# Query loads for two groups at once, with the output store ahead of them and the key loads behind them, all in SyncE's queue

## The chip, the cores and the metric

The kernel runs on one core of one Trainium2 chip. The metric is the device time of one execution in microseconds (us); the program is launched once, and there is no arithmetic on the host. A core has five engines that matter here: PE (TensorE, matrix products; its weight loads are shown as PEld), DVE (VectorE), ACT (ScalarE), POOL (GpSimd) and SP (SyncE, which only issues transfers). Transfers between HBM and SBUF, and the transposes of 16-bit tiles from SBUF to SBUF, are run by 16 DMA engines. SP issues them through one hardware queue (q1 in the profile), ACT through another (q10).

## What is computed

```python
# q: 4 x 12288 x 128, kv: 4 x 384 x 32 x 128, all float32
kv_pool = kv.reshape(B, H // 4, 4, W // 4, 4, C).mean(axis=(2, 4))
k = v = kv_pool.reshape(B, -1, C) @ w_sr            # 4 x 768 x 128
s = (q @ k.transpose(0, 2, 1)) / np.sqrt(C)
a = np.exp(s - s.max(-1, keepdims=True))
a /= a.sum(-1, keepdims=True) + 1e-09
x = (a @ v).reshape(4 * 12288, 128)
h = x @ w_in                                        # 1024 wide
e = np.exp(h - h.max(-1, keepdims=True))
solu = h * e / (e.sum(-1, keepdims=True) + 1e-09)
mu, var = solu.mean(-1, keepdims=True), solu.var(-1, keepdims=True)
out = ((solu - mu) / np.sqrt(var + 1e-06) * g_ln) @ w_out
```

An attention over 768 pooled keys, and behind it a feed-forward layer with a SoLU and a layer norm, for each of 49,152 tokens.

## The kernel before

The tokens are cut into 384 tiles of 128. Four tiles make a group (96 groups), 96 tiles make one image of the batch (4 images). One Python loop over 384 slots writes the whole program out; each engine runs its instructions in the order in which this loop emits them, so that order is set by hand. In slot t the loop emits different stages of several tiles at once:

- tile t: the scores `s` on PE (`scores_pe`, L587), their maximum on DVE, the exponential on ACT (`scores_exp`), and the split of the result into two 16-bit halves `phl` (`scores_split`), the last step of which is a DMA transpose of `phl` into `pT` (L622) that SP issues;
- the group whose last tile was two slots earlier starts its weighted sum of the values, `xa` (`values`, L647). Its products read all four `pT` of the group, so the fourth transpose of a group is the one that is needed soonest;
- tile t-10: the hidden layer `h` (L700), its maximum (`junkd`, L708), its exponential `e` (L724), the product `u` (L738), the square sum (`junk`, L803);
- tile t-11: `u` in two 16-bit halves on POOL (`uhl`, L755 and L762) and their transpose into `uT` (L777, SP);
- tile t-14: the last product `o` (L828), which reads `uT`; for every fourth tile the output `ob` (L851, DVE) and its store (L860, SP).

The queries of a group are one load of 128 x 512 floats (256 KB) into `qf` (`q_load`, L528, SP; three buffers). It is issued at the end of the last slot of each group, three groups ahead.

The keys of image b+1 are summed up while image b is worked on: 16 positions `pos`, each one load `kv_load` (L227) of 128 x 768 floats (384 KB) into `kv`, and for `pos` above 0 two additions on POOL into `ka` (`kv_add`, L238), one for each half. `kv_plan` gives the slot of each step. Of the image that follows the first, six loads are issued by SP at the start (`SOON`); the other 42 loads of the kernel are issued by ACT, in a slot that is a multiple of four. Of these the two of table `LATE` have slots of their own. From slot 70 of an image on, the steps of `key_steps` make the keys and values of the next image out of `ka`.

The order in which all this reaches SP is shown with the change. SP works through its queue strictly in order: a transfer whose input is not ready holds all that stand behind it. At most eight transfers of both queues are under way, since each waits for the one that used its semaphore eight transfers earlier.

The functions that the diff touches, and those that call them:

Of the kernel before, what the change touches and what calls it, by code (L numbers as in the profile page):

```python
# [11 lines left out]
F32 = mybir.dt.float32  # L12
# [9 lines left out]
P = 128  # L22
# [9 lines left out]
GT = 4  # L32
# [11 lines left out]
LO = 14  # L44
# [17 lines left out]
FIT_AT = 302  # L62

SOON = {0: (), 1: (8, 8), 2: (8, 8), 3: (27, 33), 4: (39, 45), 5: (51, 54)}
LATE = {6: (12, 16, 18), 7: (16, 20, 22)}


@with_exitstack
def kernel(
# [15 lines left out]
    nc = tc.nc  # L85

    dmt = ctx.enter_context(tc.tile_pool(name="dmt", bufs=2))
# [59 lines left out]
    state = {}  # L147
# [351 lines left out]
    def kv_plan(b):  # L499


        for pos in range(RR):


            if b == 1 and pos in SOON:
                for half, slot in enumerate(SOON[pos]):
                    yield slot, [partial(kv_add, b, half, pos)]
                continue
            slot = 6 * pos - (28 if b == 1 else 30)
            load, *adds = (slot // GT * GT, slot + 3, slot + 5)  # L510
            if b == 1 and pos in LATE:
                load, *adds = LATE[pos]
            yield load, [partial(kv_load, b, pos)]
            if pos:
                for half, add in enumerate(adds):
                    yield add, [partial(kv_add, b, half, pos)]
        for slot, half, *fs in key_steps(b):
            yield slot, [partial(f, b, half) for f in fs]


    QL = 1

    def q_load(g):
        if g >= NG or g % QL:
            return
        b, gb = divmod(g, GPB)
        t = dmt.tile([P, QL * 512], F32, tag="qf", name=f"qf_{g}", bufs=3)
        nc.sync.dma_start(t, qT[b, :, gb * 512 : (gb + QL) * 512])  # L528
        state["qf", g // QL] = t

    def by_tile(a):
        return a.rearrange("p (t j) -> p j t", j=GT)
# [4 lines left out]
    def wide(g):  # L537
        return g < GPB or g >= NG

    def q_scale(g):  # L540
        if wide(g) or NG <= g:
            return
        qf = state["qf", g // QL][:, (g % QL) * 512 : (g % QL + 1) * 512]
        nc.gpsimd.tensor_scalar(
# [3 lines left out]
    def q_split(g):  # L548
        if NG <= g < NG + GPB:
            return  # L550
        qf = state["qf", g // QL][:, (g % QL) * 512 : (g % QL + 1) * 512]
        if wide(g):
# [292 lines left out]
        nc.gpsimd.tensor_tensor(f, f2, state.pop(("v3", g)), op=ALU.add)  # L845
        nc.gpsimd.tensor_tensor(f2, f, mhalf[:, :GT], op=ALU.pow)

    def final_out(g, to=None):
        _, f = state["f", g]
        ob = dmt.tile([P, GT, P], F32, tag="ob", name=f"ob_{g}")  # L850
        nc.vector.scalar_tensor_tensor(  # L851
            ob,
            state["po", g].rearrange("p (j c) -> p j c", j=GT),
            swi,
            f.unsqueeze(2).to_broadcast([P, GT, P]),
            op0=ALU.mult,
            op1=ALU.mult,
        )
        rows = out[g * GT * P : (g + 1) * GT * P, :] if to is None else to
        nc.sync.dma_start(rows.rearrange("(p j) c -> p (j c)", j=GT), ob.rearrange("p j c -> p (j c)"))  # L860

# [32 lines left out]
    for n in range(16):  # L894
        if n == OUT_AT:
            nc.sync.dma_start(raw_out, w_out.bitcast(I32))
        if n == Q_AT:
            q_load(0)
        kv_first_load(*divmod(n, 8))
    q_load(1)  # L900
    for pos in SOON:
        kv_load(1, pos, nc.sync)
    nc.scalar.mul(w_sr16, wsr, 1.0 / RR)
# [157 lines left out]
    def at_last(t, fn, *args):  # L1061

        if 0 <= t < NT and t % GT == GT - 1:
            fn(t // GT, *args)
# [13 lines left out]
    for slot in range(NT):  # L1078
        i = slot - LH
# [50 lines left out]
        if slot < NT - 1:  # L1130
            at(slot - LO, final_pe)
        at(i - 1, hidden_turn)
        if slot % GT == GT - 1:
            q_load(slot // GT + 3)
        at_last(slot - LO - 1, final_out)
        at_last(slot - XSP, values_out)
        for st in todo:
            if st[0].func is kv_add:
# [96 lines left out]
    def general():  # L1235

        for b in range(B):
# [4 lines left out]
            for n in range(16):  # L1242
# [4 lines left out]
                t = dmt.tile([P, NK], F32, tag="kvc", name=f"kvg_{kb}_{n}", bufs=9)  # L1247
# [9 lines left out]
            kv_now(kb, kv_v_pe, kv_v_out, kv_v_high, kv_v_low)  # L1257
            g = kb * GPB
            with tc.For_i(0, GPB, 1) as i:
                qf = dmt.tile([P, 512], F32, tag="qf", name=f"qf_{g}", bufs=3)  # L1260
                nc.sync.dma_start(qf, qT[b, :, bass.ds(i * 512, 512)])
                state["qf", g] = qf
                q_split(g)
                q_low(g)
                for t in range(g * GT, g * GT + GT):
                    scores_pe(t)
                    scores_exp(t)
                    scores_split(t)
                for n in range(8):
                    values(g, n // 2, n % 2)  # L1270
                values_out(g)
                values_split(g)
                values_norm(g)
                values_recip(g)
                values_recip_u(g)
                for t in range(g * GT, g * GT + GT):
                    hidden_pe(t)
                    hidden_max(t)
                    hidden_exp(t)
                    hidden_u(t)  # L1280
                    hidden_high(t)
                    hidden_low(t)
                    hidden_turn(t)
                    hidden_var(t)
                    final_pe(t)
                final_scale(g)
                final_root(g)
                final_out(g, to=out[bass.ds(b * NTOK + i * 512, 512), :])
# [39 lines left out]
```

## Time and profile before

| what | us |
|---|---|
| median of 3 runs | 1852.11 |
| lowest and highest of them | 1843.84, 1857.69 |
| the profiled execution, its own time | 1843.65 |
| its span (first to last instruction) | 1841.9 |
| PE busy in it | 1818.3 |
| DVE, ACT, POOL busy | 1761.9, 1742.6, 1667.2 |

The profiled execution took 1.75 us more than its span, and it is 8.5 us under the median of the unprofiled runs, at their lower end. Busy times overlap, since the engines work beside each other. An engine's busy share is an average; which engine holds a stretch up is read from the chain of waits, and from how far apart the same step of two groups that follow each other stands.

### The profile page before, as it was taken

Reading aid. Unit: us, or ns where it says so; the run is one execution under the profiler, and the core shown is the slowest. Engines: PE = TensorE matmul, PEld = TensorE weight load, DVE = VectorE, ACT = ScalarE, POOL = GpSimd, SP = SyncE. Lnnn points to the kernel's source line nnn. Section 1 sums busy time; section 2 is a strip of 40 time slices with the busy share of each in tenths; the row PEclk is TensorE's granted clock in tenths of the full one; section 3 lists DMA queues with packets and bytes.
Section 4 is the critical chain, followed back from the end, with each engine's and each line's share of the span. In section 5 each row is a group of like instructions: output and inputs, shape, how many; then the busy total and the mean of one; then the engine's idle time right before and its main releaser. Section 6 shows DMA issues by size and latency. Waiting matters only on the chain.

```text
span 1841.9 us, 42770 instructions
## 1 busy us (share of the span) xinstructions
PE 1818.3 (99%) x15747; PEld 1218.5 (66%) x15747; DVE 1761.9 (96%) x2635; ACT 1742.6 (95%) x3129; POOL 1667.2 (91%) x1466
## 2 busy tenths in 40 slices
PE   8999999999999999999999999999999999999998
PEld 5577777777666666666666666666666666666666
DVE  6999999999999999999999998999999999999997
ACT  5999999999999999999999998999999999999997
POOL 5899999899999999989999998998988988888887
PEclk9999999999999999999999999999999999999999
DMA  9999999999999999999999999999999999999997
GB/s 301 203 249 230 230 253 232 247 230 237 242 241 241 246 245 242 246 235 235 247 239 241 242 222 230 247 239 224 222 233 230 232 235 231 220 235 224 230 223 168
DMA packets 1440027, 432.80 MB, mean 235 GB/s; under 512 B 1404608, under 2 KB 1408832, under 8 KB 1439552
## 3 DMA queue, kind: packets, MB, share of 16 engines
q1 hardware_dynamic: 1433616, 413.45, 112.6%
q10 hardware_dynamic: 6192, 16.52, 3.2%
q8 instruction: 126, 2.06, 0.5%
q14 instruction: 93, 0.76, 0.1%
HBM read 52.50 MB, written 25.17 MB: 42 GB/s over the span
## 4 chain that ended last, share of the span: by engine, by line
PE 46%; DVE 26%; ACT 15%; issue 9%; DMA 2%; POOL 1%; SPq 0%; DVEq 0%; ACTq 0%; POOLq 0%
PE o L828 13%; PE h L700 13%; PE s L587 10%; PE xa L647 10%; DVE junkd L708 8%; DVE phl L619 6%; DVE nm L608 5%; ACT e L724 4%; ACT junk L803 4%; DVE u L738 3%; ACT phl L611 3%; ACT s L609 2%; DVE ob L851 2%; DVE xl L659 2%; DMA kv<-in_kv_dram 1%
## 5 line engine op out<-in xcount | busy, mean ns | idle before, releaser
L762 POOL TENSOR_TENSOR uhl<-u,uhl 128x1024 f16<-128x1024 f32 x382 | 815.0, 2134 | 32.3 <-ACT uhl L753 0.6
L828 PEld LDWEIGHTS <-uT 128*128 128x128 f16 x9072 | 537.9, 98 | 89.1 <-issue 0.9
L828 PE MATMUL o<-wch,uT 128*128 128x128 f16 x6048 | 568.1, 219 | 0.1
L828 PE MATMUL o<-wcl,uT 128*128 128x128 f16 x3024 | 526.1, 219 | 0.0
L738 DVE SCALAR_TENSOR_TENSOR u<-h,rz,e 128x1024 f32<-128x1024 f32 x384 | 490.4, 1277 | 33.3 <-ACT e L724 32.7
L708 DVE TENSOR_SCALAR_CACHE_REDUCE junkd<-h,rz 128x1024 bf16<-128x1024 f32 x384 | 490.7, 1278 | 7.6 <-PE h L700 7.2
L647 PE MATMUL xa<-pT,vhl 128*128 128x512 f16 x1728 | 470.4, 380 | 5.4 <-DMA pT<-phl 5.4
L755 POOL TENSOR_SCALAR uhl<-u 128x1024 f16<-128x1024 f32 x379 | 395.8, 1044 | 83.9 <-DVE u L738 72.7
L724 ACT ACTIVATE e<-h,nm,rz 128x1024 f32<-128x1024 f32 x384 | 458.5, 1194 | 8.2 <-DVE junkd L708 8.2
L803 ACT ACTIVATE junk<-u,su 128x1024 bf16<-128x1024 f32 x384 | 438.0, 1141 | 0.1
L609 ACT ACTIVATE s<-s,nm 128x768 f32<-128x768 f32 x384 | 334.7, 872 | 47.6 <-DVE nm L608 47.1
L619 DVE SCALAR_TENSOR_TENSOR phl<-s,phl 128x768 f16<-128x768 f32 x384 | 365.8, 953 | 6.5 <-ACT phl L611 4.1
L608 DVE TENSOR_REDUCE nm<-s 128x1 f32<-128x768 f32 x384 | 360.1, 938 | 9.1 <-PE s L587 4.6
L611 ACT ACTIVATE phl<-s 128x768 f16<-128x768 f32 x384 | 311.1, 810 | 12.1
L700 PEld LDWEIGHTS <-xh 128*128 128x128 f16 x1536 | 144.0, 97 | 195.4 <-issue 27.1
L647 PEld LDWEIGHTS <-vhl 128*128 128x128 f16 x1728 | 162.4, 98 | 141.3 <-issue 16.0
L700 PE MATMUL h<-w_in_h,xh 128*128 128x512 f16 x768 | 228.9, 380 | 3.6 <-DVE rz L682 3.2
L700 PE MATMUL h<-w_in_l,xh 128*128 128x512 f16 x768 | 229.0, 380 | 0.0
L700 PE MATMUL h<-w_in_h,xl 128*128 128x512 f16 x768 | 228.8, 380 | 0.0
L587 PEld LDWEIGHTS <-qh 128*128 128x128 f16 x1152 | 122.6, 114 | 42.9
L587 PE MATMUL s<-kh,ql 128*128 128x384 f16 x576 | 140.8, 326 | 0.1
L587 PE MATMUL s<-kl,qh 128*128 128x384 f16 x576 | 140.8, 326 | 0.0
(153 smaller groups left out, 1820.4 us busy)
## 6 DMA issues: line engine op xcount, KB each, us to landing
qf<-in_q_dram SPq DMA_DIRECT2D x96, 256.0 KB, 3.8
out_dram<-ob SPq DMA_DIRECT2D x96, 256.0 KB, 2.9
kv<-in_kv_dram ACTq DMA_DIRECT2D x42, 384.0 KB, 4.3
kv<-in_kv_dram SPq DMA_DIRECT2D x22, 384.0 KB, 7.5
pT<-phl SPq DMA_TRANSPOSE x384, 4.0
uT<-uhl SPq DMA_TRANSPOSE x378, 4.6
raw_in<-in_moe_w_in_dram SPq DMA_DIRECT2D x1, 1024.0 KB, 5.1
raw_out<-in_moe_w_out_dram SPq DMA_DIRECT2D x1, 1024.0 KB, 9.6
```

Source lines behind the costliest of these rows:

```text
L587: nc.tensor.matmul(s[:, half, :384], tokens(lh)[:, j, :], rh[:, half * 384 : (half + 1) * 384], start=n == 0, stop=n == 2,)
L608: nc.vector.tensor_reduce(nm, s, axis=AX.XY, op=ALU.max, negate=True)
L619: nc.vector.scalar_tensor_tensor(phl[:, 1], state.pop(("s", t)), SC, phl[:, 0], op0=ALU.mult, op1=ALU.subtract)
L647: nc.tensor.matmul(xa, v[:, c, :], pT[:, :, a * NKC + c, :], start=n == 0, stop=n == len(seq) - 1)
L700: nc.tensor.matmul(h[:, hs], lh[:, ts], rh[:, hs], start=n == 0, stop=n == 2)
L708: nc.vector.tensor_scalar(junk, state["h", t], state["rz", g][1][:, j : j + 1], None, op0=ALU.mult, op1=ALU.min, accum_out=nm,)
L724: nc.scalar.activation(e, state["h", t], AF.Exp, bias=nm, scale=state["rz", g][0][:, js], accum_out=state["z2", g][:, js],)
L738: nc.vector.scalar_tensor_tensor(u, state.pop(("h", t)), state["rz", g][2][:, j : j + 1], state.pop(("e", t)), op0=ALU.mult, op1=ALU.mult, ...
L755: nc.gpsimd.tensor_scalar(uhl[:, 0, :], u, 1.0, 1.0, op0=ALU.mult, op1=ALU.mult)
L762: low.tensor_tensor(uhl[:, 1, :], u, uhl[:, 0, :], op=ALU.subtract)
L803: nc.scalar.activation(junk, u, AF.Square, scale=-float(DFF), bias=su, accum_out=state["v3", g][:, j : j + 1],)
L828: nc.tensor.matmul(po[:, ts], uT[:, a * NFC + c, :], w[:, c, :], start=start, stop=stop)
```

## The change

Queries are loaded for two groups at once (`QL = 2`; 512 KB, 128 x 1024 floats, two buffers in the place of three), every eight slots, at slot 8n+3. The store of a group's output is taken out of `final_out` and emitted one slot later, so that it stands directly ahead of the query load (and in the other half of the groups at the same place, with no load behind it). The loads of the keys are all issued by SP, in the same slots, one or two of them directly behind the query load; `kv_plan` moves some of the additions of `ka` two slots later, so that they stay at least four slots behind their load, and the two rows of `LATE` get other slots. The first two groups' queries are still loaded separately, into two halves of one tile.

```diff
-LATE = {6: (12, 16, 18), 7: (16, 20, 22)}
+LATE = {6: (11, 16, 18), 7: (19, 22, 24)}
...
             slot = 6 * pos - (28 if b == 1 else 30)
-            load, *adds = (slot // GT * GT, slot + 3, slot + 5)
+            load = (slot - 2) // (2 * GT) * 2 * GT + GT - 1
+            first = max(slot + 3, load + GT)
+            adds = first, first + 2
             if b == 1 and pos in LATE:
                 load, *adds = LATE[pos]
-            yield load, [partial(kv_load, b, pos)]
+            yield load, [partial(kv_load, b, pos, nc.sync)]
...
-    QL = 1
+    QL = 2
...
-        t = dmt.tile([P, QL * 512], F32, tag="qf", name=f"qf_{g}", bufs=3)
+        t = dmt.tile([P, QL * 512], F32, tag="qf", name=f"qf_{g}", bufs=2)
...
+    def q_first_load(g):
+        if g == 0:
+            state["qf", 0] = dmt.tile([P, QL * 512], F32, tag="qf", name="qf_0", bufs=2)
+        nc.sync.dma_start(
+            state["qf", 0][:, g * 512 : (g + 1) * 512], qT[0, :, g * 512 : (g + 1) * 512]
+        )
...
-    def final_out(g, to=None):
+    def final_out(g, to=None, later=False):
...
+        state["ob", g] = ob
+        if not later:
+            final_store(g, to)
+
+    def final_store(g, to=None):
+        ob = state.pop(("ob", g))
         rows = out[g * GT * P : (g + 1) * GT * P, :] if to is None else to
         nc.sync.dma_start(rows.rearrange("(p j) c -> p (j c)", j=GT), ob.rearrange("p j c -> p (j c)"))
...
-            q_load(0)
+            q_first_load(0)
...
-    q_load(1)
+    q_first_load(1)
...
-        if slot % GT == GT - 1:
-            q_load(slot // GT + 3)
-        at_last(slot - LO - 1, final_out)
+        at_last(slot - LO - 2, final_store)
+        if slot % (2 * GT) == GT - 1:
+            q_load(slot // GT + 4)
+        at_last(slot - LO - 1, partial(final_out, later=True))
```

In SyncE's queue, in the second image before the change, a row `pT_8210` is one of the four transposes of one group's `phl` (the number is that of the buffer's tile), and `uT`, `out_dram`, `qf` are the transfers named above:

```order
L860 DMA out_dram<-ob_8106 128x512
L622 DMA_TRANSPOSE pT_7919<-phl_8112 128x12x128
L777 DMA_TRANSPOSE uT_8176<-uhl_8128 128x16x128
L528 DMA qf_8178<-in_q_dram 128x512
L622 DMA_TRANSPOSE pT_8210<-phl_8183 128x12x128
L777 DMA_TRANSPOSE uT_8244<-uhl_8196 128x16x128
L622 DMA_TRANSPOSE pT_8210<-phl_8252 128x12x128
L777 DMA_TRANSPOSE uT_8322<-uhl_8269 128x16x128
L622 DMA_TRANSPOSE pT_8210<-phl_8331 128x12x128
L777 DMA_TRANSPOSE uT_8393<-uhl_8343 128x16x128
L860 DMA out_dram<-ob_8395 128x512
L622 DMA_TRANSPOSE pT_8210<-phl_8401 128x12x128
```

The store stands directly ahead of the fourth `pT` of each group, and the query load directly ahead of the first; the same place in the queue after the change:

```order
L875 DMA out_dram<-ob_7787 128x512
L631 DMA_TRANSPOSE pT_7890<-phl_7863 128x12x128
L786 DMA_TRANSPOSE uT_7924<-uhl_7876 128x16x128
L631 DMA_TRANSPOSE pT_7890<-phl_7932 128x12x128
L786 DMA_TRANSPOSE uT_8002<-uhl_7949 128x16x128
L631 DMA_TRANSPOSE pT_7890<-phl_8011 128x12x128
L786 DMA_TRANSPOSE uT_8073<-uhl_8023 128x16x128
L631 DMA_TRANSPOSE pT_7890<-phl_8080 128x12x128
L786 DMA_TRANSPOSE uT_8144<-uhl_8096 128x16x128
L875 DMA out_dram<-ob_8075 128x512
L530 DMA qf_8147<-in_q_dram 128x1024
L227 DMA kv_8_8149<-in_kv_dram 128x768
```

Now all plain loads and stores stand in one place of the queue, between the `uT` that follows a group's fourth `pT` and the first `pT` of the next group (a second `kv` load follows the last row shown here), and nothing but transposes stands between the first `pT` and the fourth.

On ACT, in the stretch of the first image where the keys of the next one are made, one of the 42 loads stands so before the change (`xh` is the copy of `xa`, `s` and `phl` the exponential and the split of the scores, `junk` and `e` belong to the hidden layer):

```order
L724 ACTIVATE e_5866,z_18_5654<-h_5805,nm_74_5863,rz_5632 128x1024
L654 ACTIVATE xh_5907<-xa_5645,sv_115 128x512
L227 DMA kv_3_5911<-in_kv_dram 128x768
L609 ACTIVATE s_5851,z_all<-s_5851,nm_5913 128x2x384
L611 ACTIVATE phl_5916<-s_5851 128x768
L803 ACTIVATE junk_5936,v_18_5655<-u_5918,su_5919 128x1024
```

After the change the same place of ACT's order has the activations alone:

```order
L733 ACTIVATE e_5847,z_18_5633<-h_5783,nm_74_5844,rz_5611 128x1024
L663 ACTIVATE xh_5888<-xa_5624,sv_115 128x512
L618 ACTIVATE s_5832,z_all<-s_5832,nm_5892 128x2x384
L620 ACTIVATE phl_5895<-s_5832 128x768
L812 ACTIVATE junk_5915,v_18_5634<-u_5897,su_5898 128x1024
```

ACT loses its 42 DMA rows and nothing else moves on it; the orders of PE and DVE are those of before, and on POOL only some additions into `ka` stand later, by two slots.

## Rows read from the trace of the kernel before

**Rows 1.** The page: busy time of each engine, its share of the span, instructions.

```profile
PE 1818.3 (99%) x15747; PEld 1218.5 (66%) x15747; DVE 1761.9 (96%) x2635; ACT 1742.6 (95%) x3129; POOL 1667.2 (91%) x1466
```

**Rows 2.** Timeline of DVE, one row a group: start us, us, line and operation.

```profile
674.07 0.74 DVE L851 SCALAR_TENSOR_TENSOR ob<-o,swi,f 128x512 f32<-128x512 f32 x1
692.45 0.74 DVE L851 SCALAR_TENSOR_TENSOR ob<-o,swi,f 128x512 f32<-128x512 f32 x1
...
1082.28 0.74 DVE L851 SCALAR_TENSOR_TENSOR ob<-o,swi,f 128x512 f32<-128x512 f32 x1
1103.08 0.74 DVE L851 SCALAR_TENSOR_TENSOR ob<-o,swi,f 128x512 f32<-128x512 f32 x1
...
1144.29 0.74 DVE L851 SCALAR_TENSOR_TENSOR ob<-o,swi,f 128x512 f32<-128x512 f32 x1
1162.92 0.74 DVE L851 SCALAR_TENSOR_TENSOR ob<-o,swi,f 128x512 f32<-128x512 f32 x1
```

**Rows 3.** Chain of waits from 600 to 700 us, its shares by line.

```profile
by line: PE o L828 29.1%; PE h L700 28.8%; PE xa L647 21.4%; PE s L587 20.8%
```

**Rows 4.** Chain of waits from 1080 to 1145 us: start us, us, what.

```profile
1091.24 7.05 DMA pT<-phl
...
1130.85 7.04 DMA pT<-phl
```

**Rows 5.** Timeline of SP, the issues around two groups' ends.

```profile
1130.22 0.53 SPq L860 DMA_DIRECT2D out_dram<-ob  x1
1130.85 1.66 SPq L622 DMA_TRANSPOSE pT<-phl  x1
...
1137.34 0.57 SPq L528 DMA_DIRECT2D qf<-in_q_dram  x1
...
1151.36 1.46 SPq L622 DMA_TRANSPOSE pT<-phl  x1
...
1158.11 2.30 SPq L777 DMA_TRANSPOSE uT<-uhl  x1
```

**Rows 6.** Timeline of ACT: the key loads nearest to those two `pT`.

```profile
1131.67 0.34 ACTq L227 DMA_DIRECT2D kv<-in_kv_dram  x1
...
1154.56 0.34 ACTq L227 DMA_DIRECT2D kv<-in_kv_dram  x1
```

**Rows 7.** Tile `pT`, the transpose issued at 1130.85: issue to landing.

```profile
DMA to landing us min/median/max: 7.0/7.0/7.0
```

**Rows 8.** Tile `kv`, the load issued at 1131.67: issue to landing.

```profile
DMA to landing us min/median/max: 5.9/5.9/5.9
```

**Rows 9.** Tile `pT`, the transpose issued at 1151.36: issue to landing.

```profile
DMA to landing us min/median/max: 3.6/3.6/3.6
```

**Rows 10.** Tile `uT`, the transpose issued at 1158.11: issue to landing.

```profile
DMA to landing us min/median/max: 6.2/6.2/6.2
```

**Rows 11.** Windows: busy us of each engine (instructions), granted PE clock, DMA share, GB/s.

```profile
794.00:813.00 19.00, 19.00 (x169) 12.66 (x168) 17.87 (x28) 18.64 (x38) 16.18 (x15) 1.00 1.16 229
...
1130.50:1131.50 1.00, 1.00 (x7) 0.53 (x6) 1.00 (x2) 1.00 (x3) 0.92 (x2) 1.00 1.28 290
1133.50:1134.50 1.00, 1.00 (x17) 0.90 (x15) 1.00 (x2) 1.00 (x2) 0.83 (x3) 1.00 1.29 73
1138.00:1140.00 2.00, 2.00 (x6) 0.71 (x7) 0.10 (x2) 1.95 (x4) 1.77 (x3) 0.60 1.14 283
```

**Rows 12.** Timeline of PE: the first reads of what landed after 1151.36 and 1158.11.

```profile
1157.96 0.59 PE L647 MATMUL xa<-pT,vhl 128*128 128x512 f16 x2
...
1169.49 0.22 PE L828 MATMUL o<-wch,uT 128*128 128x128 f16 x1
```

**Rows 13.** Line L227, ACT's issues of key loads: ns min/median/max, first and last start us.

```profile
L227 ACTq DMA_DIRECT2D kv<-in_kv_dram x42: 334/335/365, 66.5 to 1191.2; - x42
```

**Rows 14.** Chain of waits from 44 to 50 us.

```profile
45.03 1.28 PE s L587 x6
46.32 2.17 PE xa L647 x10
```

## Prediction of the time after the change

> **What bounds the kernel now.** The page comes first. PE is busy for 99% of the span, with DVE and ACT close behind [rows 1]. Such shares say that little is left, not where it is, so the next view is a step that comes once a group: the start of `ob` on DVE. In a quiet stretch two of them stand 692.45 - 674.07 = 18.38 us apart [rows 2]. The chain of waits of such a stretch runs through PE alone [rows 3], so a group cannot be shorter while PE's work stays what it is. The stretch from 1082 to 1163 us is different: the next distances are 20.80 us, 41.21 us for two groups, and 18.63 us, together 80.64 for four [rows 2]. Four quiet groups would take 73.52, so 7.1 us were lost there.
>
> The chain of waits of that stretch tells to what: twice it goes through the landing of a `pT`, 7.05 and 7.04 us after its issue [rows 4]. Both are the fourth transpose of their group, issued right behind the store [rows 5]. One group later the same transpose landed in 3.6 us, at 1155.0 [rows 5, 9]; PE read it at 1157.96 [rows 12]. It had 3.0 us to spare, and a landing after 7 us uses up all of that. PE then waits, and behind the wait it runs for a while at a granted clock of 0.60 [rows 11], which adds to the loss. The first of the two made its group 2.4 us longer, the second the two groups around it 4.4 us.
>
> What made these two late? Beside the second, ACT had issued a load of keys at 1131.67, 0.8 us behind the transpose; that load landed after 5.9 us, at 1137.6, and the transpose at 1130.85 + 7.0 = 1137.9, right behind it [rows 5 to 8]. In the group after it ACT's load was issued at 1154.56, 3.2 us behind the `pT`, which had landed in time [rows 6, 9]. While transposes run alone, 290 GB/s move; two us after ACT's load was issued, 73 GB/s moved [rows 11]. So a transpose that is under way when ACT's load enters is slowed down until that load has landed. Mostly that hits a `uT`, which has time; it hits a fourth `pT` when SP is a little late.
>
> **The change, part by part.**
>
> *Key loads from ACT to SP.* No load enters from the side any more; all 42 [rows 13] stand in SP's queue behind the query load and ahead of a first `pT`. The two late landings go: -7.1 us. What is late next there is the fourth `pT` itself at its usual 3.6 us, with 3.0 to spare.
>
> *The store one slot later.* It leaves the place directly ahead of the fourth `pT`. That takes 0.53 us of issue [rows 5] and 256 KB, 0.9 us at 290 GB/s [rows 11], out of the way of the one transfer that is needed soonest. PE doesn't wait there in a quiet group, so it is worth 0 in the sum and up to 1.4 us of margin. The store itself is waited for by nobody but the buffer of the next but one `ob`.
>
> *SP's own time.* Query loads fall from 96 to 49: 47 x 0.57 = 27 us less [rows 5]. The 42 key loads add between 42 x 0.34 = 14 us (their price on ACT, [rows 13]) and 42 x 0.57 = 24 us (that of a query load on SP); I take the upper end, since the engine is the same. Net 3 us less for SP, worth 0: SP isn't on PE's path in a quiet group.
>
> *The block of loads.* Every eighth slot, 256 KB of store, 512 KB of queries and one or two times 384 KB stand together. Before, the store and 256 KB of queries stood ahead of the second transpose behind this place too, so what is new for it is 256 KB + 2 x 384 KB = 1.02 MB at most, 3.5 us at 290 GB/s. That second transpose is a `uT`; the one issued at 1158.11 landed after 6.2 us, at 1164.3, and was first read at 1169.5 [rows 5, 10, 12]: some 5 us to spare. 3.5 us fit, so the cost is 0, by a cover of 1.5 us. The fourth `pT` comes three slots (13.8 us) later. A slot has 18.38 / 4 = 4.6 us, and its two transposes move 384 + 512 KB, 3.2 us at 290 GB/s; up to 1.4 us a slot can be made up, 4.2 in three. So the block is mostly worked off, and what is left is no more than the 0.9 us that the store gave back. Without the two covers, each such block costs what a late landing costs now (2.4 or 4.4 us).
>
> *ACT without the 42 issues.* 42 x 0.335 = 14 us of ACT's time [rows 13]. In quiet groups PE sets the pace, so nothing of it shows. Where the next image's keys are made, ACT is busy for 18.64 of 19.00 us [rows 11] and stands in the chain; four of the loads fall into each of the first two such stretches (the third image has no next but one), 8 x 0.335 = 2.7 us at most, 0 at least. DVE and PE are as full there [rows 11], so I take half: -1.3 us.
>
> *The start and POOL.* 256 KB more stand ahead of the first transposes (0.9 us at 290 GB/s). The first `xa` follows the scores on PE without a gap, 45.03 + 1.28 = 46.31 [rows 14], so no transfer holds it: 0, at most 0.9. Additions that stand two slots later are the same work and aren't read before slot 70: 0.
>
> **Sum**, against the profiled execution: span 1841.9 - 7.1 - 1.3 = 1833.5, and with 1.75 us around the span 1835.3 us. The median of the runs shown is 8.5 us above the profiled one, which is two to four more late landings at 2.4 to 4.4 us each; they go by the same reason, so the new median should be near the new profile. I leave half of one landing (1.2 us) for whatever else makes a transfer late and forecast **1836.5 us**, 0.8% under 1852.11. Its own range is 1832 to 1842. One per cent (18.5 us) is about what a measurement of this kernel can tell from no change; the bound for faster is 1833.6.
>
> **Rivals.**
>
> *The late landings stay (the same, about 1849).* If it is the bytes and not the second queue that make a transpose late, the loads do the same from SP's queue, and the waits return elsewhere. For it: the load and the transpose share the DMA engines in either case. Against it: 73 GB/s where transposes alone have 290 [rows 11] is too little for mere sharing. All that is left then is ACT's 1.3 us and half the store's margin: 1844 to 1853, near the median of now. The Trainium skill, "DMA: Bandwidth & Descriptors", section "Issuing engines are not separate DMA queues", speaks for this rival and against the change: transfers run on the same 16 DMA engines whichever engine issues them, and spreading only saves issue time. By that rule moving the loads buys nothing and the time stays at about 1849 us, in the place of the forecast's 1836.5. The trace so far disagrees, with the two landings of 7 us right behind a load of the other queue [rows 5 to 8].
>
> *The blocks come too late (slower, 1862 to 1884).* There are 11 blocks with two key loads. If the 512 KB query load and the two loads behind it take over 5 us more than now, the `uT` behind them is late for `o`, each time at 2.4 to 4.4 us with the clock's fall: 26 to 48 us on top of 1836. For it: a cover of only 1.5 us in the group shown. Against it: 5 us would need 1.02 MB at 204 GB/s.
>
> *More than the two landings (faster, about 1832).* If ACT alone sets the pace at the image boundaries, all of the 2.7 us goes, and if nothing is ever late any more the 1.2 us isn't needed: 1841.9 - 7.1 - 2.7 + 1.75 = 1833.9, and a start that is a little shorter brings it under the bound. For it: ACT's 18.64 of 19. Against it: DVE with 17.87 and PE with 19.00 beside it [rows 11].
>
> That the change doesn't do what it says is excluded for the order: SyncE's rows show it.
>
> **Chances.** Forecast 0.58, landings stay 0.17, blocks too late 0.07, more than that 0.18. Faster by over 1%: 0.18 and a tenth of all from the forecast's lower end, 0.28. Slower by over 1%: 0.07. The rest, 0.65, within 1%. For 8 in 10 the range takes the forecast, the faster case and the greater part of the unchanged one: 1830 to 1852.
>
> **What would show it.** In the changed profile no group outside the image boundaries of the later images is longer than 18.4 us; no `pT` stands in the chain of waits with 7 us; `xa` waits for no DMA; the granted clock stays at 1.00 in mid-run; the stretches where keys are made are 0 to 1.3 us shorter each. PE waiting for `uT` behind a block would show the second rival, and PE waiting for `pT` at its old places the first. I am wrong on the whole if the runs' spread (1844 to 1858) has another source than late transposes: then the profile loses its 7 us and the median doesn't follow.

## The result, and the profile after

The changed kernel takes 1868.58 us (median of 6 runs, 1863.98 to 1870.68), beside 1849.11 (6 runs, 1841.72 to 1857.69) of the kernel before in the same call. The ratio is 1.0105, 95% interval 1.0076 to 1.0134: slower by about one per cent, where 0.8% faster was forecast. The profiled execution has a span of 1866.5 us and a time of its own of 1868.39, so this profile is a typical one.

First the page of the kernel after: busy times, the chain of waits by engine and by line, and the issues of transfers (number, size, median us from issue to landing).

```profile
PE 1823.0 (98%) x15747; PEld 1219.1 (65%) x15747; DVE 1767.5 (95%) x2635; ACT 1746.1 (94%) x3129; POOL 1667.8 (89%) x1466
...
PE 40%; DVE 26%; ACT 14%; issue 9%; DMA 8%; POOL 2%; SPq 0%; DVEq 0%; ACTq 0%; POOLq 0%
PE o L837 11%; PE h L709 11%; PE xa L656 9%; PE s L596 8%; DVE junkd L717 8%; DMA pT<-phl 8%; DVE phl L628 6%; DVE nm L617 5%; ACT e L733 4%; DVE u L747 4%; ACT junk L812 4%; ACT phl L620 3%; ACT s L618 2%; DVE xl L668 2%; DVE ob L860 2%
...
kv<-in_kv_dram SPq DMA_DIRECT2D x64, 384.0 KB, 6.7
...
qf<-in_q_dram SPq DMA_DIRECT2D x47, 512.0 KB, 5.3
```

The work is the same as in [rows 1] to within 0.3%; the span is 24.6 us longer. What is new is `pT` with 8% in the chain: landings of transposes now set the pace again and again. The starts of `ob`, the answer to [rows 2], show where. DVE's timeline of the kernel after, in image 1 and in image 3:

```profile
551.05 0.74 DVE L860 SCALAR_TENSOR_TENSOR ob<-o,swi,f 128x512 f32<-128x512 f32 x1
...
569.44 0.74 DVE L860 SCALAR_TENSOR_TENSOR ob<-o,swi,f 128x512 f32<-128x512 f32 x1
...
589.50 0.74 DVE L860 SCALAR_TENSOR_TENSOR ob<-o,swi,f 128x512 f32<-128x512 f32 x1
...
1408.89 0.75 DVE L860 SCALAR_TENSOR_TENSOR ob<-o,swi,f 128x512 f32<-128x512 f32 x1
...
1427.28 0.74 DVE L860 SCALAR_TENSOR_TENSOR ob<-o,swi,f 128x512 f32<-128x512 f32 x1
```

The group from 551.05 is quiet, 18.39 us. The next one, which has two key loads in its block, takes 20.06. In image 3, where no keys are loaded any more, every group of its stretch from 1335 to 1813 us takes 18.38 to 18.40, block or not. Laid beside the kernel before by such steps, the first 20 groups (image 0) lost 3.1 us, the next 23 (image 1) 14.0, the next 21 (image 2) 5.1, the 27 after them 0.1; the start 0.3 and the end 1.9 make up the rest of the 24.6. Such sums come from one execution each; in e8, below, images 0 and 1 are the same program, and one of them differs by 6 us from this execution.

Two views of the long group. SP's timeline in the kernel after, from 561 us:

```profile
561.90 0.58 SPq L875 DMA_DIRECT2D out_dram<-ob  x1
562.53 0.42 SPq L530 DMA_DIRECT2D qf<-in_q_dram  x1
563.00 0.95 SPq L227 DMA_DIRECT2D kv<-in_kv_dram  x2
564.06 2.23 SPq L631 DMA_TRANSPOSE pT<-phl  x1
566.38 5.87 SPq L786 DMA_TRANSPOSE uT<-uhl  x1
572.34 1.42 SPq L631 DMA_TRANSPOSE pT<-phl  x1
...
575.59 1.52 SPq L631 DMA_TRANSPOSE pT<-phl  x1
...
579.42 1.52 SPq L631 DMA_TRANSPOSE pT<-phl  x1
...
584.31 0.57 SPq L875 DMA_DIRECT2D out_dram<-ob  x1
584.99 1.47 SPq L631 DMA_TRANSPOSE pT<-phl  x1
```

The chain of waits there, in order of time (start us, us, what), which answers to [rows 4]:

```profile
564.06 8.51 DMA pT<-phl
...
572.65 0.81 ACT phl L620
...
579.42 5.18 DMA pT<-phl
...
584.85 1.24 PE xa L656 x5
```

The block goes out in 2.0 us of issues, but the `pT` behind it takes 8.5 us to land, and the issue of the `uT` after it takes 5.87 us, in which SP issues nothing else. It isn't its input that it waits for: POOL had finished that `uhl` (L771) at 562.0. So the next `pT` is issued at 572.34. DVE had finished its `phl` at 564.36 + 0.95 = 565.31:

```profile
564.36 0.95 DVE L628 SCALAR_TENSOR_TENSOR phl<-s,phl 128x768 f16<-128x768 f32 x1
...
568.57 0.95 DVE L628 SCALAR_TENSOR_TENSOR phl<-s,phl 128x768 f16<-128x768 f32 x1
...
573.49 0.96 DVE L628 SCALAR_TENSOR_TENSOR phl<-s,phl 128x768 f16<-128x768 f32 x1
...
578.50 0.95 DVE L628 SCALAR_TENSOR_TENSOR phl<-s,phl 128x768 f16<-128x768 f32 x1
```

I call that distance the **lag** of a `pT`, and the table further down has its means. Here it is 572.34 - 565.31 = 7.0 us, one slot later 575.59 - 569.52 = 6.1, then 579.42 - 574.45 = 5.0, and behind the next store 584.99 - 579.45 = 5.5. The third is the fourth `pT` of its group: it lands at 584.60, and PE, which needs it, stands still for 1.55 us. Over the whole span the waits for `pT` read (us, times, longest):

```profile
ACT phl L620 <- DMA pT<-phl: 13.7, 17, 1.8
...
PE xa L656 <- DMA pT<-phl: 10.4, 9, 1.6
...
PEld L656 <- DMA pT<-phl: 7.4, 7, 1.8
```

### The profile page after: what moved, and what is told of

Read it like the earlier page. It is cut to its first block, busy times and chain, and to the rows that moved or that the text cites. A ratio compares the mean times of both kernels' runs of the same rounds, so it can differ in the third digit from the quotient of the medians.

```text
span 1866.5 us, 42646 instructions
## 1 busy us (share of the span) xinstructions
PE 1823.0 (98%) x15747; PEld 1219.1 (65%) x15747; DVE 1767.5 (95%) x2635; ACT 1746.1 (94%) x3129; POOL 1667.8 (89%) x1466
## 4 chain that ended last, share of the span: by engine, by line
PE 40%; DVE 26%; ACT 14%; issue 9%; DMA 8%; POOL 2%; SPq 0%; DVEq 0%; ACTq 0%; POOLq 0%
PE o L837 11%; PE h L709 11%; PE xa L656 9%; PE s L596 8%; DVE junkd L717 8%; DMA pT<-phl 8%; DVE phl L628 6%; DVE nm L617 5%; ACT e L733 4%; DVE u L747 4%; ACT junk L812 4%; ACT phl L620 3%; ACT s L618 2%; DVE xl L668 2%; DVE ob L860 2%
## 5 line engine op out<-in xcount | busy, mean ns | idle before, releaser
L771 POOL TENSOR_TENSOR uhl<-u,uhl 128x1024 f16<-128x1024 f32 x382 | 814.9, 2133 | 32.3 <-ACT uhl L762 0.7
L596 PE MATMUL s<-kh,qh 128*128 128x384 f16 x576 | 140.9, 326 | 0.0
```

Source lines behind the costliest of these rows:

```text
L596: nc.tensor.matmul(s[:, half, :384], tokens(lh)[:, j, :], rh[:, half * 384 : (half + 1) * 384], start=n == 0, stop=n == 2,)
L771: low.tensor_tensor(uhl[:, 1, :], u, uhl[:, 0, :], op=ALU.subtract)
```

## Experiments

Two theories stood against each other in several forms. One, called "path" or "block" in the expectations: something in the new order (what stands directly ahead of a `pT`, the length of the block) makes that transpose late. The other, called "room": while keys are loaded, the DMA engines have hardly more room than a group of 18.38 us needs, and any order of the copies but a lucky one runs out of it. Further rivals ("buffer", "compute", "place", "entries", "burst") are told in the expectations that name them. Each ratio below is to the kernel before in the same call.

### The parts of the change, one by one

**e1_act**: the kernel after, with its key loads issued by ACT in the changed slots.

```
-            yield load, [partial(kv_load, b, pos, nc.sync)]
+            yield load, [partial(kv_load, b, pos)]
```

> The changed kernel with the 42 key loads issued by ACT again, in the changed slots; everything else stays (queries for two groups, store one slot later, additions). Theory path (a key load in SyncE's own queue takes that queue's time in full, and SyncE then runs 3 to 7 us behind for as long as keys are loaded): about 1840 to 1850 us, SyncE's issues 1 to 3 us behind their producers. Theory block (it is that store, queries and keys stand together, whoever issues them): 1860 to 1868. Theory buffer (the first transpose behind the block holds one of three phl buffers too long): about 1860, since the block of store and 512 KB of queries stays and ACT's loads come in on top.

Measured: 1876.55 us, ratio 1.0147 [1.0079, 1.0216]. That is above all three ranges. In the changed slots issuing from ACT doesn't help, so the issuing engine isn't what made the change slow.

**e2_sp**: the kernel before with nothing but the key loads moved to SP, in their old slots (the same line the other way round).

> The kernel before with the 42 key loads issued by SP in place of ACT, in the slots of before, one at a time; no blocks. Theory path: slower than before, 1858 to 1870 us. Theory block: as before or a little faster, 1838 to 1850, and no landing of 7 us. Theory buffer: as before, since single loads of 384 KB hold a phl buffer no longer than a query load does.

Measured: 1860.20 us (10 runs), ratio 1.0082 [1.0055, 1.0108]. This is the edit that was to win 7.1 us, alone, and it loses 0.8%. It lies in the range of "path" (1858 to 1870), which had the loads take SP's time in full; "block" and "buffer" are missed.

**e3_phl4**: the kernel after with a fourth buffer for `phl`, so that ACT needn't wait for a `pT` that is under way.

```
-            state["vt", b] = dmt.tile([P, 2, 2, 384], F16, tag="vt", name=f"vt_{b}", bufs=1)
+            state["vt", b] = dmt.tile([P, 2, 2, 384], F16, tag="kvc", name=f"vt_{b}", bufs=9)
...
-        phl = dmt.tile([P, 2, 2, 384], F16, tag="phl", name=f"phl_{t}", bufs=3)
+        phl = dmt.tile([P, 2, 2, 384], F16, tag="phl", name=f"phl_{t}", bufs=4)
```

> The changed kernel with four phl buffers in place of three (vt moves into the buffers of the key loads to make room). Theory buffer: ACT's 13.7 us of waits for a landed pT go, and 1845 to 1852 us are reached, the rest being PE's waits for the fourth pT. Theory path: ACT's waits go, but SyncE stays 3 to 7 us behind and PE waits for the fourth pT all the more: 1860 to 1870. Theory block: between, 1855 to 1862.

Measured: 1869.12 us, ratio 1.0109 [1.0038, 1.0179], no other than the kernel after. The list of its waits has ACT's wait for `pT` no more, and the same transposes are waited for by PE:

```profile
PEld L656 <- DMA pT<-phl: 12.5, 7, 3.2
...
PE xa L656 <- DMA pT<-phl: 12.3, 10, 2.0
```

So the buffer only decided who waits. That theory falls; the time is in the range of "path" (1860 to 1870).

**e4_store**: the kernel before with the store alone one slot later.

```
+        at_last(slot - LO - 2, final_store)
         if slot % GT == GT - 1:
             q_load(slot // GT + 3)
-        at_last(slot - LO - 1, final_out)
+        at_last(slot - LO - 1, partial(final_out, later=True))
```

> The kernel before with only the output's store one slot later, so that it no longer stands directly ahead of a group's fourth pT. All three theories: no slower than before, 1838 to 1850 us; the fourth pT has 0.6 to 1.4 us more to spare, so that if late fourth pT are what spreads the runs of before (1842 to 1858), the spread shrinks and the median falls to 1836 to 1843. If nothing changes, that margin is not what decides.

Measured: 1860.73 us (10 runs, 1847.68 to 1869.02), ratio 1.0048 [1.0015, 1.0081]. All three theories had 1838 to 1850 here, and all three were wrong.

**e7_ql2**: the kernel before with the query pairs alone.

```
-    QL = 1
+    QL = 2
...
-        if slot % GT == GT - 1:
-            q_load(slot // GT + 3)
+        if slot % (2 * GT) == GT - 1:
+            q_load(slot // GT + 4)
```

> The kernel before with the query pairs alone: one load of 512 KB every eight slots in place of 256 KB every four, at the same place on the queue; store and key loads as before. Theory 'room': the same bytes, somewhat burstier: 1843 to 1856, lag 2 to 4 us in images 1 and 2. Theory 'path': the fourth pT of every second group waits behind twice the bytes and lands 0.9 us later than behind one load, 24 times, of which a part shows: 1850 to 1865. If it is near 1837, the pairs take pressure off, since the transposes meet copies half as often.

Measured: 1861.13 us (10 runs), ratio 1.0067 [1.0041, 1.0093]. The time is in the range of "path" and above that of "room", the lag (2.4 and 3.3 us) in that of "room". So each of the three parts alone costs 0.5 to 0.8%. They sum to 2.0%, and all three together cost 1.05%: these are not three separate prices.

**e13_noblock**: the kernel after with the key loads one at a time, in the slots of before, by SP.

```
-            load = (slot - 2) // (2 * GT) * 2 * GT + GT - 1
-            first = max(slot + 3, load + GT)
-            adds = first, first + 2
+            load, *adds = (slot // GT * GT, slot + 3, slot + 5)
```

> The changed kernel with its key loads one at a time in the slots of before, by SP: query pairs and the later store stay, the block of loads is gone. Theory 'block' (the length of the block is the cause): most of the loss is won back, 1846 to 1856. Theory 'room' (any order of the copies but one or two runs into the same lack of room, the block or not): 1858 to 1872, lag of 3.5 to 5 us in images 1 and 2.

Measured: 1870.80 us, ratio 1.0120 [1.0082, 1.0159]. With the block gone nothing is won back, as "room" had it.

**e10_shift**: the kernel before with its key loads, still by ACT, one slot later.

```
-            yield load, [partial(kv_load, b, pos)]
+            yield load + 1, [partial(kv_load, b, pos)]
```

> The kernel before with the key loads one slot later in the group, still by ACT and one at a time: they then come two slots behind the query load instead of one, and one slot ahead of the store instead of two. Theory 'room': the load stands close to another copy either way; the sum per group is the same, so 1842 to 1862, wherever its coincidences fall. Theory 'place' (the slot of before is the one in which nothing waits for the queue, and any other costs): 1855 to 1870, as in the kernels where the store, the key loads or the query loads alone were moved.

Measured: 1880.39 us (1870.85 to 1887.57), ratio 1.0171 [1.0130, 1.0211]: the slowest of all that do the same work, worse than "room" (1842 to 1862) and "place" (1855 to 1870) allowed. The place of a copy matters, then, and the one of before is a good one; why this one is so bad isn't settled.

### The bytes

**e5_before_nokeys** and **e6_after_nokeys**: the kernels before and after without the 42 key loads.

```
+    def kv_same(b, pos):
+        state["kv", b, pos] = state["kv", 1, 5]
...
-            yield load, [partial(kv_load, b, pos)]
+            yield load, [partial(kv_same, b, pos)]
```

> The kernel before without its 42 key loads behind the first six: the sums, the projection and all else stay, and read the sixth tile again in place of those left out. Theory 'room': while keys are loaded the DMA engines have hardly more room in a group than PE's 18.38 us, and it is the bytes that make transposes late. Then the lag of a transpose behind its producer falls from 1.5 to 2.2 us in images 1 and 2 to that of image 3 (0.4 to 0.7), no group of images 1 and 2 is long, and the time is 1834 to 1838, the 7.1 us of the four late groups gone. Theory 'compute': the long groups come with the work on the keys (GpSimd's additions, the projection, its weights on TensorE), which images 1 and 2 alone have: the lag stays at 1.5 and more and the time within 1 per cent of 1848.

> The changed kernel without its 42 key loads, everything else of the change in place (pairs of queries, the store one slot later, the later additions). Theory 'room': no bytes, no loss: 1834 to 1840, as the kernel before without them, lag 0.4 to 1.2 us in every image. Theory 'path' (store directly ahead of a query load of twice the size, on the path of the fourth pT): the 47 blocks without key loads still make that pT late in images 1 and 2: 1845 to 1865, with waits for pT left at the slots of the blocks.

With these keys the program's own test of its ranges sends it, after the 96 groups, into its exact fallback loop, so the whole times (7376.77 and 7399.37 us) say nothing here. The 96 groups are done before that, and the last `ob` of DVE's timeline ends the comparison. Without key loads, the kernel before:

```profile
1829.06 0.75 DVE L854 SCALAR_TENSOR_TENSOR ob<-o,swi,f 128x512 f32<-128x512 f32 x1 [3.79 <-PE o L831]
```

Without key loads, the kernel after:

```profile
1831.14 0.75 DVE L863 SCALAR_TENSOR_TENSOR ob<-o,swi,f 128x512 f32<-128x512 f32 x1 [3.79 <-PE o L840]
```

With the loads, the kernel after:

```profile
1858.45 0.75 DVE L860 SCALAR_TENSOR_TENSOR ob<-o,swi,f 128x512 f32<-128x512 f32 x1 [3.79 <-PE o L837]
```

The kernel before has its own at 1835.79. So leaving out the loads wins 6.7 us before, the 7.0 of the late groups of image 2, and 27.3 us after. All else of the change is still in e6: it costs 2.1 us, of which 1.4 lie at the start. "Compute" falls, since e5 and e6 still do the work on the keys.

**e8_image3**: the kernel after with 16 more loads of the key size in image 3, into tiles that nobody reads.

```
+    for pos in range(RR):
+        slot = 6 * pos - 30
+        load = (slot - 2) // (2 * GT) * 2 * GT + GT - 1
+        plan.setdefault((B - 1) * TPB + load, []).append([partial(kv_dummy, pos)])
```

> The changed kernel with 16 more loads of the key size in the last image, placed as the plan would for a fifth image; they fill key tiles that nobody reads. Theory 'room': image 3, without a loss so far, now loses as images 1 and 2 do, +1 to +2.4 us in each group with such a block, some 8 of them at a mean 1.4: 1877 to 1888, lag in image 3 from 1.0 to 3.5 to 5 us. Theory 'compute': nothing but bytes is added, so image 3 stays at 18.38 us a group and the time at 1866 to 1871.

Measured: 1877.73 us, ratio 1.0162 [1.0113, 1.0211], 9 us over the kernel after, in the range of "room". In its profile the groups of image 3, which lost under 1 us together in every other kernel, are 14.3 us longer than those of the kernel after. Images 0 and 1 are the same program in both, and differ by +3.5 and -6.1 us.

**e11_nostore**: the kernel after with its blocks, pairs and key loads, and four stores in place of 96.

```
+        if to is None and g % 24 != 23:
+            return
```

> The changed kernel with its key loads and query pairs, but the output stored for every 24th group alone (four of 96 stores of 256 KB are left; the rest of the output is not written). Theory 'room': 262 KB a group fewer, as many as the key loads bring, so it is worth what leaving out the key loads was worth: 1834 to 1846, lag 0.6 to 1.5 us in images 1 and 2, though the blocks with one or two key loads are still there. Theory 'block' (768 KB to 1.28 MB of loads in one piece ahead of a uT and a pT make that pT late): the blocks lose only the 256 KB of the store at every second one, the groups with key loads stay long, 1855 to 1866.

Measured: 1837.42 us (1837.25 to 1838.51, 6 runs), ratio 0.9931 [0.9904, 0.9957]. The blocks with one and two key loads are all there, and cost nothing that can be seen as soon as 256 KB a group of something else are gone. The runs' spread is 1.3 us where the kernel before has 24 in the same call.

### Smaller pieces

**e9_halves**: the kernel before with each key load in two halves, two slots apart, by ACT. **e12_halves_q**: the query loads halved as well.

```
-            yield load, [partial(kv_load, b, pos)]
+            yield load, [partial(kv_load, b, pos, half=0)]
+            yield load + 2, [partial(kv_load, b, pos, half=1)]
... (e12 also)
+            q_load(slot // GT + 3, (0,))
+        if slot % GT == 1 and slot > GT:
+            q_load(slot // GT + 2, (1,))
```

> The kernel before with each of the 42 key loads in two halves of 196 KB, both issued by ACT, the second two slots (9.2 us) behind the first; the bytes are the same. Theory 'room': the bytes of a group stay, but the burst that has to fit between two transposes is half as long, so the occasional long groups of images 1 and 2 get fewer: 1837 to 1846, lag in image 2 from 2.3 to 1.5 us, and a narrower spread than 1837 to 1866. Rival 'entries': each load that comes in costs the transpose under way a fixed delay, whatever its size; with 84 in place of 42 the lag grows and the time is 1850 to 1865.

> The kernel of the halved key loads with the query loads in halves as well: 128 KB in the slot of before and 128 KB two slots later, the bytes the same. Theory 'room': the engines carry the same sum, so no more than the occasional coincidence can be won: 1838 to 1848, lag in images 1 and 2 not under 1.5 us. Theory 'burst' (it is the longest copy behind one another that makes a transpose late): 1836 to 1840, lag under 1 us and no long group. Theory 'entries' (each load that comes in costs something of its own): 1850 to 1865.

Measured: e9 1846.39 us (12 runs, 1843.19 to 1848.92), ratio 0.9982 [0.9958, 1.0005], which can't be told from the kernel before; e12 1857.78 us (10 runs), ratio 1.0056 [1.0027, 1.0084]. For e9 "room" had 1837 to 1846 and a narrower spread, which is 5.7 us here beside 24; but the lag of image 2 was to fall to 1.5 us and is 2.8. For e12 "room" and "burst" are missed, and the time lies in the range of "entries" (1850 to 1865), in which e9 with its 42 further loads does not lie: a price for each further load isn't shown by the two together, nor excluded for the halved query loads. Shorter bursts don't help as such, and finer pieces in other slots are one more order that loses. No version that still does all the work beat the kernel before.

### What the DMA engines carried, and where SP's queue pauses

In the table of windows, the last numbers are the granted PE clock, the DMA engines' share and GB/s; the number behind the length is PE's busy time. Three stretches of 310 us, in image 1, image 2 and image 3, of the kernel before:

```profile
500.00:810.00 310.00, 310.00 (x2731) 204.25 (x2730) 303.21 (x454) 298.49 (x543) 290.99 (x255) 1.00 1.20 242
960.00:1270.00 310.00, 304.58 (x2679) 200.53 (x2677) 296.40 (x442) 292.63 (x531) 283.81 (x251) 0.99 1.19 235
1400.00:1710.00 310.00, 310.00 (x2727) 203.47 (x2726) 303.97 (x455) 298.38 (x540) 274.66 (x241) 1.00 1.18 230
```

Of the kernel after:

```profile
500.00:810.00 310.00, 300.12 (x2633) 195.67 (x2632) 293.09 (x436) 287.75 (x518) 279.90 (x248) 1.00 1.19 233
960.00:1270.00 310.00, 300.77 (x2640) 197.03 (x2638) 295.46 (x438) 289.94 (x522) 282.55 (x249) 1.00 1.19 235
1400.00:1710.00 310.00, 310.00 (x2730) 203.53 (x2729) 303.95 (x455) 298.35 (x541) 274.36 (x243) 1.00 1.17 231
```

Of the kernel after without stores (e11):

```profile
500.00:810.00 310.00, 309.94 (x2730) 204.34 (x2729) 303.48 (x455) 298.61 (x543) 291.30 (x255) 1.00 1.18 229
```

Of the kernel after with loads in image 3 (e8):

```profile
1400.00:1710.00 310.00, 302.28 (x2646) 197.34 (x2644) 297.63 (x444) 291.49 (x525) 267.19 (x237) 1.00 1.21 235
```

Without key loads a PE that never waits takes 229 to 231 GB/s. Sixteen key loads of 393 KB in an image of 24 groups of 18.38 us add 14, so with them it takes 243 to 245 in the first stretch. In the second, where the loads end (between 1185 and 1227 us), nine loads stand against eleven, and it takes 240 to 242. The kernel before carried 242 and 235, the ten other orders of the same bytes 230 to 241. This rate can't rise above what PE asks for, so it says how far PE kept its pace, and not how much the DMA engines could carry. Over shorter stretches the kernel before carried more:

```profile
256.50:293.30 36.80, 36.80 (x319) 26.15 (x318) 35.77 (x55) 35.98 (x64) 35.00 (x30) 1.00 1.19 259
594.00:741.00 147.00, 147.00 (x1298) 96.62 (x1296) 144.16 (x217) 141.51 (x257) 139.83 (x124) 1.00 1.21 247
```

What is full is better seen on SP, whose rows are its issues. This is SP in the middle of image 1 of the kernel before:

```profile
602.65 1.40 SPq L622 DMA_TRANSPOSE pT<-phl  x1
604.22 3.24 SPq L777 DMA_TRANSPOSE uT<-uhl  x1
607.54 0.54 SPq L860 DMA_DIRECT2D out_dram<-ob  x1
608.18 1.47 SPq L622 DMA_TRANSPOSE pT<-phl  x1
609.75 1.73 SPq L777 DMA_TRANSPOSE uT<-uhl  x1
611.53 0.57 SPq L528 DMA_DIRECT2D qf<-in_q_dram  x1
```

Each issue starts some 0.1 us behind the end of the one ahead of it. In the 310 us of image 1 the issues of transposes take 274 us of SP, those of copies 19, the short steps between them 13, and real pauses (over 0.2 us between two issues) come to 1.3 us. The table gives those pauses for each kernel, and the lag, both over the same three stretches of one profile each (the lag is the mean of a `pT`'s issue minus the end of its `phl` on DVE):

| kernel | GB/s, image 1 / 2 | PE busy of 310 us, image 1 / 2 | mean lag, image 1 / 2 / 3 (us) | SP's pauses of 310 us, image 1 / 2 / 3 |
|---|---|---|---|---|
| before | 242 / 235 | 310.0 / 304.6 | 1.7 / 2.4 / 0.5 | 1.3 / 4.3 / 14.5 |
| e9 halves | 239 / 241 | 307.3 / 308.4 | 3.0 / 2.8 / 0.5 | 0.9 / 2.6 / 13.5 |
| e7 pairs alone | 237 / 236 | 306.0 / 303.8 | 2.4 / 3.3 / 1.9 | 4.2 / 1.5 / 7.9 |
| e2 SP alone | 233 / 239 | 298.3 / 304.1 | 5.0 / 4.2 / 0.5 | 0.8 / 1.9 / 16.9 |
| e4 store alone | 230 / 236 | 299.4 / 300.9 | 3.7 / 3.7 / 0.6 | 0.7 / 1.2 / 15.6 |
| after | 233 / 235 | 300.1 / 300.8 | 5.0 / 5.0 / 1.0 | 0.8 / 0.7 / 12.9 |
| e3 four `phl` | 235 / 234 | 301.4 / 300.4 | 5.0 / 4.9 / 0.9 | 0.8 / 0.7 / 12.3 |
| e12 halves of queries too | 239 / 232 | 306.6 / 298.4 | 3.3 / 4.6 / 2.0 | 1.2 / 0.8 / 2.1 |
| e1 ACT, new slots | 230 / 230 | 295.9 / 297.0 | 4.6 / 5.1 / 1.0 | 2.1 / 0.8 / 11.5 |
| e13 no block | 235 / 236 | 298.9 / 301.8 | 5.1 / 4.6 / 0.9 | 0.8 / 0.8 / 11.2 |
| e10 shift | 230 / 233 | 298.7 / 299.9 | 4.8 / 4.7 / 0.4 | 0.8 / 0.8 / 21.5 |
| e8 loads in image 3 | 238 / 237 | 303.6 / 301.3 | 4.5 / 4.7 / 4.9 | 0.8 / 0.7 / 1.3 |
| e5 before, no keys | 229 / 228 | 310.0 / 309.6 | 0.4 / 0.6 / 0.7 | 27.1 / 19.7 / 11.5 |
| e6 after, no keys | 231 / 228 | 310.0 / 309.6 | 1.2 / 1.0 / 0.9 | 10.5 / 15.0 / 11.8 |
| e11 after, no stores | 229 / 227 | 309.9 / 309.6 | 1.5 / 1.4 / 0.3 | 9.2 / 19.2 / 40.7 |

So "room" holds in this form: wherever keys are loaded beside all the stores, SP has at most 4.3 us of pauses in 310, in the kernel before too, and without the keys or the stores it has 9 to 27 in images 1 and 2. Image 3 has 8 us and more (2.1 in e12), until e8 loads keys there. The other transfers also make SP's own issues longer: in e5 the eleven loads that are gone from image 1 were ACT's, and SP's transposes (one more than before) take 253 us of issue in the place of 274. How much of an issue is SP's own work and how much waiting for the DMA engines, no run here separates.

## Why the prediction was wrong

*Key loads from ACT to SP* (-7.1 us): failed. Both late landings do lie beside a load of ACT's (issued at 1092.1 and 1131.7), but the loads did it by being there, not by the queue that they came through: from SP, in the same slots, they cost 0.8% (e2), and leaving them out wins 6.7 us (e5). This is the first rival's reason. The row of 73 GB/s [rows 11], which spoke against that rival, doesn't show the load's bytes at work: in that microsecond, from 1133.5 to 1134.5, only SP's queue (q1) began packets (packets, MB, share), and the load's began at 1134.6:

```profile
q1 hardware_dynamic: 285, 0.07, 129.3%
```

What slowed the transposes there stays open. The rule named with that rival (the Trainium skill, "DMA: Bandwidth & Descriptors", section "Issuing engines are not separate DMA queues") was right that another queue buys nothing. Its other half, that a second engine saves the time of issuing, fits what the move lost: in image 1 SP had 1.3 us of pauses, and got 11 loads more to issue. That isn't all, since in the changed slots issuing from ACT wins nothing (e1).

*The block of loads* (cost 0): the step that failed by most. It held that "up to 1.4 us a slot can be made up, 4.2 in three". That counted the time of the DMA engines, at 290 GB/s, the rate of a single microsecond [rows 11], and not SP's time for issuing. In image 1 of the kernel before, 67 slots had 274 us of transposes' issues, 4.1 of 4.6 us a slot, and copies and the steps between took the rest. In image 1 of the kernel after, a block and the next stand eight slots apart, and the lags of the eight `pT` from block to block are 4.0, 6.4, 6.3, 5.3, 4.9, 4.2, 3.5 and 2.6 us (means of twelve). The block adds 3.8 us (from 2.6 to 6.4), near the 3.5 that were forecast. But that is worked off at 0.6 us a slot, and the next block comes before it is done. In the long group shown, 7.0 fell to 5.0 in two slots, where 2.8 were counted on. So the fourth `pT` behind a block goes out 5.3 us behind its `phl`, beside 1.4 in image 1 of the kernel before: 3.9 us later, with only 3.0 us to spare. Its landing, the other half of the sum, is near the 3.6 us that were forecast (median 3.9 in image 1). Without the keys, the same order has a lag of 1.2 us in image 1 (e6).

*The store one slot later* (0, with up to 1.4 us of margin): alone it costs 0.5% (e4), the query pairs 0.7% (e7). What margin it gave ahead of that `pT` shows nowhere in the time.

*SP's own time* (0): wrong where keys are loaded. The copies' issues come out as forecast (19 us of 310 before, 18 after), but the sum left out the issues of the 768 transposes, which take 1545 of the 1842 us before the change. With them SP's queue has hardly a pause, and what is put off in it reaches PE by way of `pT`. That SP's order is free in e6 holds only since SP has 10.5 us of pauses there. A single issue can also take far longer than any in [rows 5]: 5.87 us behind the block.

*ACT without the 42 issues* (-1.3): 0. Where image 2's keys are made, the two longest groups take 19.58 and 19.33 us in the kernel before, and 19.59 and 19.34 without the loads (e5), which has none of the 42 issues either.

*The start* (0 to 0.9): the first `ob` is 0.3 us later, as bounded.

*The rivals.* The measured time lies in the range of "The blocks come too late" (1862 to 1884), but not by its mechanism: PE stood for `pT`, not for a `uT`, groups with one key load lost as those with two did, and without the block the loss stays (e13). "The late landings stay" was right that the loads do the same from either queue, and had the wrong size: it counted on as many late landings as before, not on a queue that stays behind.

*What would make it wrong*, the last sentence on the runs' spread, asked the right question. The spread goes with late transposes: with room (e11) it shrinks to 1.3 us, and the lag with it. That it comes from them alone isn't shown. The way to lose it was fewer bytes, not another order.

A small slip of the sum changes nothing: 256 KB + 2 x 384 KB are 1.05 MB and 3.6 us at 290 GB/s, not 1.02 and 3.5.

**Open** is why the order of before keeps a lag of 1.7 us in image 1, with hardly more pauses than the ten others, whose lags are 2.4 to 5.1. One slot of shift (e10) is enough to lose 1.7%, and no run here explains that slot.

## What to carry to other kernels

Before you move a transfer, lay the rows of the engine that issues it end to end over a whole stage, the transposes' issues too, and look for pauses. If there are none, time that a transfer loses there is hardly made up, and another order mostly loses; what helped here was fewer bytes (0.7% faster, and a spread of 1.3 us, in the run without stores). Don't take the rate of one good microsecond for one that lasts, nor the rate that PE asks for as the most that the engines carry. A wide spread of the runs, and a lag of transfers behind their producers that is long in one stage and short in another, went with such a stage here, even where PE was busy for 99%.

## What the hardware showed that I had not expected

The DMA engines all but stop for a microsecond behind nearly every fetch of instructions. In the long group above, the windows of the kernel after read:

```profile
570.00:571.00 1.00, 1.00 (x6) 0.42 (x5) 1.00 (x3) 0.52 (x2) 1.00 (x2) 1.00 3.05 172
571.00:572.00 1.00, 1.00 (x13) 0.75 (x12) 1.00 (x2) 0.92 (x2) 0.92 (x1) 1.00 0.07 7
```

From 571 to 572 us 7 GB/s moved, with a `uT` under way. The DMA queues from 569.5 to 572 (packets, MB, share) show who came in:

```profile
q1 hardware_dynamic: 1223, 0.31, 147.0%
q8 instruction: 1, 0.02, 3.0%
```

The hole at 582 to 583 us, ahead of the second late landing, has one such packet at its start too (3 to 9 GB/s). The page counts 126 of them in 1866 us. From 100 to 1780 us there are 114, and between 0.5 and 2.0 us behind the start of one, 49 GB/s move on average; between 2.5 and 4 us behind it, 278. Of the 66 whole microseconds with under 20 GB/s, 65 lie within 2 us of such a start, in the kernel before 63 of 63. By these figures some 1.2 us of the DMA engines' time are missing behind each fetch, an estimate, and 1.5 us in a group of 18.38, which has 1.25 of them. That goes some way to why 290 GB/s don't last. The Trainium skill, "Runtime: NRT & Kernel Launch", section "Instruction fetch mechanics", says that the cost of crossing into the next block of instructions is mostly hidden. For the transfers that share the DMA engines these rows show otherwise. No run here took the fetches away, so what they cost the kernel isn't shown, nor that they are the cause of the holes and don't merely stand beside them.
